# One scan over zero-separated segments, the state kept in place, and a new order of work in a kernel that mixes a 2-D FFT filter with an S5 state space

## The chip, the cores and the metric

The kernel runs on one core of one Trainium2 chip. The metric is the device time of one execution in microseconds (us). "Span" is the length of the one profiled execution; in all runs the recorded time of an execution is its span plus about 1.7 us.

The engines are named as the profile names them: PE (matmul), PEld (weight load, overlaps PE), DVE (VectorE), ACT (ScalarE), POOL (GpSimd), SP (queues DMAs).

## The reference

The inputs are `x` (2048 x 1024, bf16), spectral weights, and the tables of an S5 layer with 1024 complex states. The output mixes two branches by a gate for each row.

```python
g = sigmoid((x * gate_w).sum(-1, keepdims=True))
a = irfft2(rfft2(x) * (w_r + 1j * w_i))              # spectral branch
Lam_bar = exp(dt * Lam)                              # S5 branch, P = 1024 states
Bu = x @ B_bar.T                                     # complex
h[t] = Lam_bar * h[t-1] + Bu[t]                      # over 2048 time steps
b = 2.0 * (h @ Cmat.T).real + x * Dskip
out = g * a + (1 - g) * b
```

## The kernel before

The state branch is cut into 16 **units** `unit(c, q)`: 256 time steps (`c` = 0 to 7) times four blocks of 128 states (`q` = 0, 1). A unit is 64 matmuls into PSUM (the "B product", tile `psu`), an eviction by ACT into `u`, then DVE work: rotate by a table so that the complex recurrence becomes a real one, scan, rotate back. The result `h` waits in one of six buffers until the C products that read it are done.

```python
def b_unit(c, q):
    u = up.tile([P, 4, 2, TC], BF16, name="u")             # two buffers; TC = 256
    for j2 in range(2):
        psu = psU.tile([P, 2, 2, TC], FP32, name="psu", tag="psu")   # psU: two buffers
        ...                                                # 32 matmuls of 128x256
        nc.scalar.copy(out=u[:, 2 * j2:2 * j2 + 2], in_=psu)
    return u

def unit(c, q):
    u = b_unit(c, q)
    ...                                                    # rotate: su, u (4 DVE operations)
    for j in range(4):
        jb = 4 * q + j
        rb = r_sb[:, jb:jb + 1].to_broadcast([P, TC])
        for ri in range(2):
            nc.vector.tensor_tensor_scan(out=u[:, j, ri, :], data0=rb, data1=u[:, j, ri, :],
                                         initial=(0.0 if c == 0 else carry[:, jb, ri:ri + 1]),
                                         op0=ALU.mult, op1=ALU.add)
    ...                                                    # carry for the next 256 steps (3 small ones)
    h = halloc(sh, BF16)                                   # six buffers, 3 + 3
    ...                                                    # rotate back: sg, h (4 DVE operations)
    hs[c, q] = h
```

The spectral branch is a generator, `gfnet`. Its stages are a first transform, then sixteen **W steps** (PE `ps_s`, ACT, DVE multiply by W, PE `ps_is`, ACT, DMA to DRAM), then an inverse stage. `pull(budget)` runs it for so many us of PE work; between pulls the source puts units in. The W loop fetches one step ahead:

```python
X3_next = s2w(0)
Ccol = fixup()
for b in range(16):
    X3 = X3_next
    if b + 1 < 16:
        X3_next = s2w(b + 1)
    psc = psA.tile([P, 2, K], FP32, name="ps_is1", tag="ps")
    ...
```

A C product of 128 rows, `c_gemm(tb)`, multiplies the two `h` tiles of its time range (`q` = 0 and 1) by the C tables into the PSUM tile `ps_y`. Four row blocks have their C products done **early**, before the spectral branch can deliver them; they go to DRAM and come back as `yl` in a "late" finish. `finish` takes eight matmuls of the last transform (`ps_id`), evicts them by ACT into a gated-output buffer `eo`, forms sum and difference `ga` on DVE, adds the state branch and writes the rows out.

```python
def c_gemm(tb):
    psy = psA.tile([P, D], FP32, name="ps_y", tag="ps")
    ...                                       # 32 ps_y matmuls of 128x512, 8 small ones by dgD
def early(tb):
    psy = c_gemm(tb)
    for hf in range(2):
        ye = fft["gq"].tile([P, K], FP32, name="ye", tag="ga")
        nc.scalar.activation(out=ye, in_=psy[:, K * hf:K * (hf + 1)], func=ACT.Copy, scale=omg[:, tb:tb + 1])
        nc.sync.dma_start(out=y_dram[tb, hf], in_=ye)

def finish(tb, psy=None):
    pse = psU.tile([P, 2, K], FP32, name="ps_id", tag="psu")     # shares the two psU buffers
    ...
    eo = raw[:, D * (4 + tb % 2):D * (5 + tb % 2)].rearrange("p (c k) -> p c k", c=2)
    nc.scalar.activation(out=eo, in_=pse, func=ACT.Copy, scale=gB[:, tb:tb + 1])
    ga = fft["gq"].tile([P, 2, K], BF16, name="ga")
    nc.vector.tensor_add(out=ga[:, 0], in0=eo[:, 0], in1=eo[:, 1])
    nc.vector.tensor_sub(out=ga[:, 1], in0=eo[:, 0], in1=eo[:, 1])
    ...                                       # add yl (late) or ps_y; DMA out
```

The last stage is a loop in which each pass has a finish, a late finish while there are any, and a unit:

```python
    pull(5.0);  unit(0, 0)
    pull(10.0); unit(1, 0)
    pull(11.6)
    pull(13.0); unit(0, 1)
    pull(14.6); unit(1, 1)
    pull(7.0);  unit(2, 0)
    pull(1e9)                                 # rest of the spectral stages
    unit(2, 1)
    after_ic()
    for tb in range(NEARLY):                  # NEARLY = 4
        early(tb)
        if tb % 2:
            for q in range(2):
                unit(3 + tb // 2, q)
    todo = list(range(NEARLY, 16)); late = list(range(NEARLY))
    for c in range(3 + NEARLY // 2, 8):
        for q in range(2):
            tb = todo.pop(0)
            finish(tb, c_gemm(tb))
            if late:
                finish(late.pop(0))
            unit(c, q)
```

The source order is not the engines' order: a scheduler places the instructions of each engine under the limits of the buffers. Where this text speaks of "the static list", it means the instruction list of PE as built.

## Time and profile before

Three runs before the prediction gave a median of 422.48 us (422.34 to 424.92). The profiled execution has a span of 424.3 us.

| stage | where it is read | before, us |
|---|---|---|
| first W step starts (first `ps_s` by K table) | times of the tile | 104.5 |
| first and last inverse product of the W steps (`ps_is` from X) | times of the tile | 123.7, 171.9 |
| last product of the inverse stage starts (`ps_is` from raw) | times of the tile | 198.8 |
| end of the span | page | 424.3 |

The page's busy times, with the share of the span and the number of instructions:

```profile
PE 373.0 (88%) x2569; PEld 237.2 (56%) x2601; DVE 301.6 (71%) x525; ACT 167.1 (39%) x210; POOL 20.9 (5%) x52
```

PE has 51 us without work. Where these lie is seen in the windows (stretch, its length, then busy us and instructions of PE, PEld, DVE, ACT, POOL, granted clock, DMA share, GB/s):

```profile
core 0: us, PE busy (x) PEld busy (x) DVE busy (x) ACT busy (x) POOL busy (x), PEclk, DMA share, GB/s
160.00:180.00 20.00, 15.17 (x91) 9.08 (x93) 19.85 (x35) 11.22 (x17) 0.00 (x0) 0.96 0.52 171
...
240.00:260.00 20.00, 19.38 (x133) 12.66 (x133) 19.69 (x30) 3.14 (x3) 0.00 (x0) 1.00 0.00 1
260.00:280.00 20.00, 14.44 (x77) 8.44 (x78) 15.21 (x25) 3.03 (x3) 0.00 (x0) 0.83 0.16 53
...
300.00:320.00 20.00, 18.23 (x121) 11.61 (x122) 17.09 (x28) 4.14 (x4) 0.00 (x0) 1.00 0.16 53
```

In the W stage DVE is full and PE is not. At 260 to 280 neither is full: PE loses 5.6 us and also part of its clock. In the later passes each window still lacks 1.8 us of PE. The waits (who waited for what, us in all, times, longest):

```profile
ACT raw L480 <- DVE ga L483: 23.4, 4, 9.1
...
PE psu L205 <- ACT raw L480: 11.6, 4, 6.0
DVE h L235 <- PE ps_y L457: 11.2, 1, 11.2
```

The timeline around the hole (start, length, engine, what, and in brackets the idle time before it and its releaser):

```profile
263.80 0.42 DVE L483 TENSOR_TENSOR ga<-raw 128x512 bf16<-128x512 bf16 x1
...
264.34 1.11 ACT L480 ACTIVATE raw<-ps_id,gB 128x1024 bf16<-128x1024 f32 x1 [9.14 <-DVE ga L483]
...
265.50 6.07 PE L205 MATMUL psu<-xT,BT 128*128 128x256 bf16 x32 [6.02 <-ACT raw L480]
```

Read from the bottom: a B product waits 6.02 us for a PSUM buffer, which the finish's `ps_id` holds until ACT has evicted it; ACT waited 9.14 us for DVE's `ga`, which reads the same `eo`. After the hole the 32 matmuls take 6.07 us where 3.5 to 3.7 are usual.

```profile
L378 PE MATMUL ps_is<-X,raw x16: 379/390/607, 123.7 to 171.9; 128*128 128x512 bf16 x16
```

The second of these groups are the scans of the first time range, which start from zero and not from a carry. The eight scans of a unit overlap at their ends: eight busy times of 0.73 us take 5.24 us.

### The profile page before, as it was taken

To read this page: it belongs to the slowest core of one execution; us is meant where nothing else is said; L and a number is where in the kernel's file an instruction comes from. 1 tells how busy PE (TensorE), PEld (TensorE's weight loads), DVE (VectorE), ACT (ScalarE), POOL (GpSimd) and SP (SyncE) were. 2 spreads that over 40 slices of the span, in tenths; PEclk is the share of its full clock that TensorE was granted. 3 is DMA by queue.
4 is the path that set the end of the run, shared out by engine and by line. 5 is a ranking of instruction groups with operands and counts; after the bars stand their busy time and mean duration, and the time that the engine had idled before them with its cause. 6 is when DMAs were issued, how large, how long until landed. Compare 5 with 4: busy or idle time off the path is not lost.

```text
span 424.3 us, 6481 instructions
## 1 busy us (share of the span) xinstructions
PE 373.0 (88%) x2569; PEld 237.2 (56%) x2601; DVE 301.6 (71%) x525; ACT 167.1 (39%) x210; POOL 20.9 (5%) x52
## 2 busy tenths in 40 slices
PE   4769888986988998699999994998898999999993
PEld 4737555554855454477455853655565576544441
DVE  3963597192998999999077499597979789862211
ACT  2778887761227667478122211212212022011111
POOL 7100011150000000000000000000000000000000
PEclk9969999998889999999999999799999999999998
DMA  7999913999106886484312000213020100000010
GB/s 214 331 188 184 231 74 91 230 214 210 52 27 224 249 248 222 130 249 129 141 49 75 26 2 0 66 35 101 0 100 25 51 25 2 25 26 25 26 49 25
DMA packets 58078, 46.38 MB, mean 109 GB/s; under 512 B 38720, under 2 KB 43200, under 8 KB 57664
## 3 DMA queue, kind: packets, MB, share of 16 engines
q1 hardware_dynamic: 57616, 45.94, 39.1%
q0 software_dynamic: 352, 0.02, 0.7%
q8 instruction: 20, 0.33, 0.3%
q14 instruction: 10, 0.08, 0.1%
q10 hardware_dynamic: 80, 0.01, 0.0%
HBM read 22.87 MB, written 14.69 MB: 89 GB/s over the span
## 4 chain that ended last, share of the span: by engine, by line
PE 46%; DVE 26%; DMA 11%; ACT 7%; issue 6%; SPq 2%; POOL 1%; ACTq 0%; DVEq 0%; POOLq 0%
PE ps_y L457 19%; PE psu L205 10%; DVE u L224 9%; PE ps_fd L253 6%; PE ps_id L477 3%; DMA BT<-in_A_x_dram 3%; ACT X L256 3%; DVE h L235 2%; DVE t L366 2%; DMA BT<-in_B_B_im_dram 2%; DVE u L217 2%; PE ps_is L395 2%; DVE sg L234 2%; PE ps_is L397 1%; DMA turn_scratch<-A 1%
## 5 line engine op out<-in xcount | busy, mean ns | idle before, releaser
L205 PE MATMUL psu<-xT,BT 128*128 128x256 bf16 x1024 | 128.0, 280 | 17.1 <-ACT raw L480 11.6
L205 PEld LDWEIGHTS <-BT 128*128 128x128 bf16 x1024 | 102.0, 100 | 41.1 <-issue 16.7
L457 PE MATMUL ps_y<-CT,h 128*128 128x512 bf16 x496 | 114.7, 379 | 0.8
L457 PEld LDWEIGHTS <-h 128*128 128x128 bf16 x512 | 49.3, 98 | 54.4 <-ACT ZT L399 0.2
L224 DVE TENSOR_TENSOR_SCAN u<-r_sb,carry,u 128x256 bf16<-128x256 f32 x112 | 74.5, 732 | 0.0
L480 ACT ACTIVATE raw<-ps_id,gB 128x1024 bf16<-128x1024 f32 x16 | 17.8, 1114 | 119.6 <-PE ps_id L477 96.2
L207 ACT CAST u<-psu 128x1024 bf16<-128x1024 f32 x32 | 32.2, 1011 | 51.1 <-PE psu L205 40.6
L216 DVE TENSOR_TENSOR su<-u,tab 128x2048 bf16<-128x2048 bf16 x16 | 19.6, 1225 | 35.5 <-ACT u L207 35.1
L253 PE MATMUL ps_fd<-G_sb,preT 128*128 128x512 bf16 x123 | 31.7, 398 | 4.9 <-ACT X L256 4.1
L477 PE MATMUL ps_id<-raw,ZT 128*128 128x512 bf16 x124 | 29.4, 379 | 0.2
L482 DVE TENSOR_TENSOR ga<-raw 128x512 bf16<-128x512 bf16 x16 | 6.7, 420 | 31.3 <-ACT raw L480 31.3
L235 DVE TENSOR_TENSOR h<-u,tab 128x2048 bf16<-128x2048 bf16 x16 | 19.5, 1219 | 11.2 <-PE ps_y L457 11.2
L253 PEld LDWEIGHTS <-preT 128*128 128x128 bf16 x128 | 18.7, 146 | 15.4 <-issue 8.9
L256 ACT CAST X<-ps_fd 128x1024 bf16<-128x1024 f32 x16 | 20.7, 1305 | 10.1 <-PE ps_fd L253 10.1
L383 ACT CAST C<-ps_is 128x1024 bf16<-128x1024 f32 x16 | 16.2, 1014 | 15.0 <-PE ps_is L381 12.9
L217 DVE TENSOR_TENSOR u<-u,tab 128x2048 bf16<-128x2048 bf16 x16 | 19.6, 1223 | 0.4
L362 ACT CAST X<-ps_s 128x1024 bf16<-128x1024 f32 x16 | 16.3, 1018 | 8.8 <-PE ps_s L360 8.8
L234 DVE TENSOR_TENSOR sg<-u,tab 128x2048 bf16<-128x2048 bf16 x16 | 19.5, 1219 | 0.1
L477 PEld LDWEIGHTS <-ZT 128*128 128x128 bf16 x128 | 12.0, 98 | 12.3
L399 ACT CAST ZT<-ps_is 128x1024 bf16<-128x1024 f32 x16 | 15.4, 1016 | 5.7 <-DMA raw<-turn_scratch 4.5
L498 PE MATMUL pt<-ident,BT 128*128 128x128 bf16 x128 | 11.3, 250 | 6.9 <-DMA BT<-in_A_x_dram 6.9
L491 DVE SCALAR_TENSOR_TENSOR ga<-ps_y,omg,ga 128x1024 bf16<-128x1024 f32 x12 | 15.4, 1284 | 1.1
(182 smaller groups left out, 427.2 us busy)
## 6 DMA issues: line engine op xcount, KB each, us to landing
BT<-in_A_x_dram SPq DMA_DIRECT2D x8, 512.0 KB, 6.3
turn_scratch<-A SPq DMA_DIRECT2D x16, 256.0 KB, 3.2
Bb<-turn_scratch SPq DMA_DIRECT2D x16, 256.0 KB, 3.3
turn_scratch<-C SPq DMA_DIRECT2D x16, 256.0 KB, 3.1
raw<-turn_scratch SPq DMA_DIRECT2D x16, 256.0 KB, 3.6
out_dram<-ga SPq DMA_DIRECT2D x16, 256.0 KB, 2.0
W_b<-in_A_w_r_dram SPq DMA_DIRECT2D x16, 128.0 KB, 3.1
W_b<-in_A_w_i_dram SPq DMA_DIRECT2D x16, 128.0 KB, 2.8
```

What stands on the lines that cost most here:

```text
L205: nc.tensor.matmul(psu[:, j, ri, :], lhsT=BT[jb][:, ri, d8, :], rhs=xT[:, d8, TC * c:TC * (c + 1)], start=(d8 == 0), stop=(d8 == 7))
L207: nc.scalar.copy(out=u[:, 2 * j2:2 * j2 + 2], in_=psu)
L216: nc.vector.tensor_mul(out=su, in0=u[:, :, ::-1, :], in1=bc(1))
L217: nc.vector.tensor_mul(out=u, in0=u, in1=bc(0))
L224: nc.vector.tensor_tensor_scan(out=u[:, j, ri, :], data0=rb, data1=u[:, j, ri, :], initial=(0.0 if c == 0 else carry[:, jb, ri:ri + 1]), o ...
L234: nc.vector.tensor_mul(out=sg, in0=u[:, :, ::-1, :], in1=bc(3))
L235: nc.vector.tensor_mul(out=h, in0=u, in1=bc(2))
L253: nc.tensor.matmul(ps[:, cls, :], lhsT=preT_A[:, cls, d4, j, :], rhs=G_sb[:, cls, d4, :], start=(d4 == 0), stop=(d4 == 3))
L256: nc.scalar.copy(out=X1.rearrange("p r (i c) -> p c r i", c=2), in_=ps.rearrange("p c (r i) -> p c r i", r=2))
L457: nc.tensor.matmul(psy[:, 512 * dh:512 * (dh + 1)], lhsT=hs[c, jb // 4][:, jb % 4, ri, P * tq:P * (tq + 1)], rhs=CT[ri][:, jb, 512 * dh:51 ...
L477: nc.tensor.matmul(pse[:, cls, :], lhsT=ZT_t[:, 4 * cls + i, tb, :], rhs=fft["Gi"][:, 4 * cls + i, :], start=(i == 0), stop=(i == 3))
L480: nc.scalar.activation(out=eo, in_=pse, func=ACT.Copy, scale=gB[:, tb:tb + 1])
```

## The change

The intent: replace eight scans of 256 by two of 1024, with a decay table `rz` whose first entry in each segment is zero (so that no state leaks from one segment into the next) and the carry, multiplied by the decay beforehand, added to the first element; put `h` where `u` was, which frees the memory for `rz`; fetch two W steps ahead; move early C products and a seventh unit into the W stage, where PE has idle time. The diff, cut to its core:

```diff
-    hpA = ctx.enter_context(tc.tile_pool(name="hpA", bufs=3, side="left"))
+    hpA = ctx.enter_context(tc.tile_pool(name="hpA", bufs=NHA, side="left"))     # NHA, NHB = 4, 2
...
+            nc.gpsimd.tensor_copy(out=rz[:, jb, :], in_=r_sb[:, jb:jb + 1].to_broadcast([P, TC]))
+            nc.gpsimd.memset(rz[:, jb, 0:1], 0.0)
...
     def unit(c, q):
-        u = b_unit(c, q)
-        sh = [P, 4, 2, TC]
+        sh = [P, 2, 4, TC]
+        u = halloc(sh, BF16)
...
-        for j in range(4):
-            ...
-            for ri in range(2):
-                nc.vector.tensor_tensor_scan(out=u[:, j, ri, :], data0=rb, data1=u[:, j, ri, :],
-                                             initial=(0.0 if c == 0 else carry[:, jb, ri:ri + 1]), ...)
+        if c:
+            nc.vector.tensor_add(out=u[:, :, :, 0], in0=u[:, :, :, 0], in1=carry[:, :, js])
+        for ri in range(2):
+            seg = u[:, ri].rearrange("p j t -> p (j t)")
+            nc.vector.tensor_tensor_scan(out=seg, data0=rz[:, js].rearrange("p j t -> p (j t)"), data1=seg,
+                                         initial=0.0, op0=ALU.mult, op1=ALU.add)
...
-        h = halloc(sh, BF16)
-        nc.vector.tensor_mul(out=h, in0=u, in1=bc(2))
+        nc.vector.tensor_mul(out=u, in0=u, in1=bc(2))
...
-        X3_next = s2w(0)
+        X3s = [s2w(0), s2w(1)]
...                                       # gt, wp: three buffers in place of two; K3, JP, dgD made later
     def early(tb):
-        psy = c_gemm(tb)
+        psy = c_gemm(tb, psU, "psu")
...
-    pull(10.0)
+    pull(7.5)
+    unit(0, 1)
+    pull(7.5)
     unit(1, 0)
-    pull(11.6)
+    pull(7.5)
+    unit(1, 1)
+    pull(20.0)
+    unit(2, 0)
     pull(13.0)
-    unit(0, 1)
-    pull(14.6)
-    unit(1, 1)
-    pull(7.0)
-    unit(2, 0)
+    early(0)
+    unit(2, 1)
+    pull(8.0)
+    early(1)
+    pull(5.0)
+    unit(3, 0)
     pull(1e9)
-    unit(2, 1)
     after_ic()
-    for tb in range(NEARLY):
-        early(tb)
-        ...
+    early(2)
+    unit(3, 1)
+    early(3)
...
-    for c in range(3 + NEARLY // 2, 8):
+    for c in range(4, 8):
         for q in range(2):
+            unit(c, q)
             tb = todo.pop(0)
             finish(tb, c_gemm(tb))
             if late:
                 finish(late.pop(0))
-            unit(c, q)
```

## The prediction

> **What bounds the kernel now.** Span 424.3 us; the page has PE busy 373.0 us (88%), DVE 301.6 (71%), ACT 167.1. The windows of 20 us show different limits by stage. Transform and W stage, 100 to 200 us: DVE is busy 18 to 19.9 of every 20 us from 120 us on, PE about 17.7; W steps come every 3.1 us (timeline). Early products, 200 to 240: PE is full (19.9). Final loop, 260 to 340: neither is full (PE 14.4 to 18.2); PE's B products wait for a PSUM buffer held by the gated output (waits: psu <- ACT raw 11.6 us, which itself waits 23.4 us for DVE ga): an iteration with a late finish takes 19.6 us for 17.9 us of PE work. From 340 on PE is full, and a tail of 6.9 us ends it.
>
> **What the change does.**
> 1. Scan: eight scans of 256 cost 5.24 us a unit (0.655 us each, back to back). The Trainium skill, "DVE: opcode table, instruction layouts, handler registers and perf-mode slots", section "Datapath and trigger behaviour", says the scan program runs at half throughput. At the 0.96 GHz of the skill's first page that is 0.533 us for 256 elements, so only about 0.12 us a scan is fixed. Estimate: a 1024 scan costs 2.25 us, two of them 4.5: only 0.7 us saved a unit, minus 0.1 for the carry addition; 16 units: about 10 us of DVE. A unit goes from 12.7 to 12.1 us. Most of DVE's saving is NOT on the chain.
> 2. h in place of u: no duration changes; the DVE wait of 11.2 us (h <- ps_y) goes; ACT's eviction now holds the wait.
> 3. Order (read from the static instruction lists): seven units instead of six and two early products stand before the inverse stage ends, so about 8 us more PE work (196 instead of 205 us) has left the last stage, filling PE's idle time (about 19 us in 40 to 200). W steps go two deep, and in mid-loop no unit's DVE work lies between them, so steps should come every 2.3 to 2.6 us instead of 3.1; there DVE (2.2 us a step), ACT (2.25) and DMA (0.79 MB a step, at the 306 GB/s that 251 GB/s at share 0.82 implies) are all close to the limit.
> 4. Against it: 58 more B products stand before the first W step, which should start at about 110 instead of 104.5 us, since the last transform steps, and so the turn through DRAM, come later; dgD (8 x 0.25 us) moves into the busy DVE stretch; constants load later.
>
> **Sum by stage.** The W steps and inverse stage end at 203 us (199.9 before): no gain, but more work done. The last stage then takes about 206 us instead of 224.4: one unit, two early products fewer, late iterations 18.7 instead of 19.6 us, and no 5.6 us hole at 260 to 280 with the slow-clock period after it (32 B products took 6.07 us there, 3.5 elsewhere). Sum 409 us of span; before's timed runs are 1.8 us under its span: about 407.
>
> **Signs.** Scan 2.2 to 2.3 us for 1024; DVE busy down by about 10 us; W steps at 2.3 to 2.6 us; first W step near 110; PE idle after 200 us from 19 down to 10 to 12 us including the tail; PE busy nearly unchanged (365 to 373).
>
> **What would make it wrong.** A scan much cheaper or dearer than half throughput; W steps that are bound by DMA latency or by the SP queue's order; h buffers (six, held from the B product on) stalling ACT and PE; the two-bank PSUM pair shared by early products and units stalling PE. If the middle stage gains as well, 400; if the W stage stalls, 415.

## More of the kernel before

The scan's group and the W steps' inverse products (in the second line: min/median/max ns, then first and last start):

```profile
L224 DVE TENSOR_TENSOR_SCAN u<-r_sb,carry,u 128x256 bf16<-128x256 f32 x112 | 74.5, 732 | 0.0
...
L224 DVE TENSOR_TENSOR_SCAN u<-r_sb,u 128x256 bf16<-128x256 f32 x16 | 10.3, 679 | 0.0
```

A W step takes (171.9 - 123.7) / 15 = 3.21 us.

## The result, and the profile after

Four runs of after have a median of 411.18 us (410.68 to 413.13), against 423.46 us (422.34 to 424.92, four runs) of before. The ratio is 0.9726 (95%: 0.9682 to 0.9771): faster by 2.7%. A ratio compares the means of all runs, so it is not quite the ratio of the medians quoted here; for after these are six (two more took 413.87 and 411.69 us). The output is correct, as in all runs below.

| | before, us | after, us | predicted, us |
|---|---|---|---|
| first W step starts | 104.5 | 109.5 | 110 |
| a W step | 3.21 | 2.65 | 2.3 to 2.6 |
| last product of the inverse stage starts | 198.8 | 203.2 | 203 (stage end) |
| from there to the end of the span | 225.5 | 208.2 | 206 |
| span | 424.3 | 411.4 | 409 |

```profile
PE 369.1 (90%) x2570; PEld 236.8 (58%) x2601; DVE 296.9 (72%) x445; ACT 169.0 (41%) x210; POOL 28.8 (7%) x68
```

The windows of after, for the same stretches:

```profile
core 0: us, PE busy (x) PEld busy (x) DVE busy (x) ACT busy (x) POOL busy (x), PEclk, DMA share, GB/s
160.00:180.00 20.00, 18.45 (x89) 8.09 (x88) 18.25 (x31) 14.30 (x22) 0.00 (x0) 1.00 0.66 219
...
240.00:260.00 20.00, 18.54 (x123) 11.71 (x124) 16.99 (x22) 4.14 (x4) 0.00 (x0) 1.00 0.18 53
260.00:280.00 20.00, 18.61 (x127) 11.86 (x127) 17.02 (x23) 4.14 (x4) 0.00 (x0) 1.00 0.16 53
...
300.00:320.00 20.00, 18.16 (x122) 11.53 (x122) 16.74 (x22) 4.14 (x4) 0.00 (x0) 1.00 0.12 41
```

The large hole is gone, but each of these windows still lacks 1.4 to 1.8 us of PE. The waits:

```profile
ACT raw L485 <- DVE ga L488: 17.3, 4, 4.6
...
PE psu L209 <- ACT raw L485: 5.7, 4, 1.7
```

The wait of DVE for `ps_y` no longer appears. The same spot in the timeline of after:

```profile
247.76 0.42 DVE L488 TENSOR_TENSOR ga<-raw 128x512 bf16<-128x512 bf16 x1
...
248.29 1.11 ACT L485 ACTIVATE raw<-ps_id,gB 128x1024 bf16<-128x1024 f32 x1 [4.26 <-DVE ga L488]
...
249.46 3.65 PE L209 MATMUL psu<-xT,BT 128*128 128x256 bf16 x32 [1.36 <-ACT raw L485]
```

It is the same chain as before, with 1.36 us of loss in place of 6.02. The scan and the W steps:

```profile
L223 DVE TENSOR_TENSOR_SCAN h<-rz,h 128x1024 bf16<-128x1024 f32 x32 | 71.8, 2279 | 0.3
```

```profile
L375 PE MATMUL ps_is<-X,raw x16: 376/379/634, 136.9 to 176.6; 128*128 128x512 bf16 x16
```

So the middle of the kernel ends 4.4 us later (203.2 against 198.8), and the rest is 17.3 us shorter; together 12.9 us. A window from 200 us to the end gives PE 204.81 us busy of 224.30 before, and 198.25 of 211.40 after. Idle time in it fell from 19.5 to 13.2 us, busy time by 6.6 us. Of the 6.6 about 2.5 are the slow clock after the hole (6.07 us for 32 matmuls against 3.5 to 3.7); the rest is work that now runs earlier (after's window still holds the last 3 us of its inverse stage, so less of it shows here than in the list). In the static list, after the last inverse product PE has 204.7 us of work left before and 196.3 after, 8.4 us less (an estimate: matmuls counted in the list, at 0.11 us for 256 columns and 0.217 us for 512, their pitch in the trace). So the 17.3 us are about 8.4 of work moved, 6.3 of idle time and 2.5 of slow clock. In the static list of before no C product stands ahead of the end of the inverse stage; in that of after 64 `ps_y` matmuls do. The trace also shows what did not move: 490 B matmuls start ahead of the end of the inverse stage in before and only 433 in after, and DVE begins the seventh unit at 190.5 us in before and at 206.2 in after. What was gained is two C products (some 14.7 us); almost one unit's B product (57 matmuls, 6.3 us) went the other way.

### The profile page after: what moved, and what is told of

The parts are those of the page before. It is cut to its first block, busy times and chain, and to the rows that moved or that the text cites. A ratio compares the mean times of both kernels' runs of the same rounds, so it can differ in the third digit from the quotient of the medians.

```text
span 411.4 us, 6415 instructions
## 1 busy us (share of the span) xinstructions
PE 369.1 (90%) x2570; PEld 236.8 (58%) x2601; DVE 296.9 (72%) x445; ACT 169.0 (41%) x210; POOL 28.8 (7%) x68
## 4 chain that ended last, share of the span: by engine, by line
PE 51%; DVE 23%; DMA 11%; ACT 8%; issue 4%; SPq 1%; POOLq 1%; ACTq 0%; POOL 0%; DVEq 0%
PE ps_y L462 18%; PE psu L209 16%; DVE h L223 5%; PE ps_fd L249 5%; PE ps_id L482 3%; ACT X L252 3%; DMA raw<-turn_scratch 2%; DMA W_b<-in_A_w_r_dram 2%; DMA Bb<-turn_scratch 2%; DVE h L216 1%; DVE su L215 1%; PE ps_is L392 1%; DVE h L232 1%; DVE sg L231 1%; DMA yl<-y_scratch 1%
## 5 line engine op out<-in xcount | busy, mean ns | idle before, releaser
L209 PE MATMUL psu<-xT,BT 128*128 128x256 bf16 x1024 | 124.0, 276 | 9.0 <-ACT raw L485 5.7
L209 PEld LDWEIGHTS <-BT 128*128 128x128 bf16 x1024 | 100.6, 99 | 30.7 <-issue 7.6
L223 DVE TENSOR_TENSOR_SCAN h<-rz,h 128x1024 bf16<-128x1024 f32 x32 | 71.8, 2279 | 0.3
L485 ACT ACTIVATE raw<-ps_id,gB 128x1024 bf16<-128x1024 f32 x16 | 17.8, 1114 | 113.8 <-PE ps_id L482 96.6
L211 ACT CAST h<-psu 128x1024 bf16<-128x1024 f32 x32 | 32.3, 1010 | 51.7 <-PE psu L209 51.7
L215 DVE TENSOR_TENSOR su<-h,tab 128x2048 bf16<-128x2048 bf16 x16 | 19.6, 1224 | 42.8 <-ACT h L211 42.6
L249 PE MATMUL ps_fd<-G_sb,preT 128*128 128x512 bf16 x122 | 29.8, 381 | 5.1 <-ACT X L252 4.3
L216 DVE TENSOR_TENSOR h<-h,tab 128x2048 bf16<-128x2048 bf16 x16 | 19.6, 1223 | 0.6
L232 DVE TENSOR_TENSOR h<-h,tab 128x2048 bf16<-128x2048 bf16 x16 | 19.6, 1223 | 0.1
L231 DVE TENSOR_TENSOR sg<-h,tab 128x2048 bf16<-128x2048 bf16 x16 | 19.5, 1219 | 0.1
L503 PE MATMUL pt<-ident,BT 128*128 128x128 bf16 x128 | 12.4, 268 | 5.8 <-DMA BT<-in_A_x_dram 5.8
L396 ACT CAST ZT<-ps_is 128x1024 bf16<-128x1024 f32 x16 | 16.1, 1012 | 3.5 <-PE ps_is L394 2.8
L392 PE MATMUL ps_is<-R_sb,raw 128*128 128x256 bf16 x64 | 14.9, 273 | 2.2 <-DMA raw<-turn_scratch 2.1
```

The source lines that it names most:

```text
L209: nc.tensor.matmul(psu[:, j, :], lhsT=BT[4 * q + j][:, ri, d8, :], rhs=xT[:, d8, TC * c:TC * (c + 1)], start=(d8 == 0), stop=(d8 == 7))
L211: nc.scalar.copy(out=u[:, ri], in_=psu)
L215: nc.vector.tensor_mul(out=su, in0=u[:, ::-1], in1=bc(1))
L216: nc.vector.tensor_mul(out=u, in0=u, in1=bc(0))
L223: nc.vector.tensor_tensor_scan(out=seg, data0=rz[:, js].rearrange("p j t -> p (j t)"), data1=seg, initial=0.0, op0=ALU.mult, op1=ALU.add)
L231: nc.vector.tensor_mul(out=sg, in0=u[:, ::-1], in1=bc(3))
```

## The experiments

The theory at the start was that the order (with the pool of the early products) gives the gain, that the scan gives a little, and that `h` in place is free. Rivals: the scan gives the gain by relieving DVE; or the W depth does. Edits are against after (names that begin with a) or before (names that begin with b). One combination could not be had: before with the long scan alone. The build refuses a scan over a two-level operand, so the scan needs the new layout, and with `u` and `h` apart the decay table leaves less room than the 32 KB a partition that the C tables need.

### a_old: after without the order

Before's order of units, its early products' pool, its W depth and its `h` pools; the new scan and `h` in place stay.

```diff
-NHA, NHB = 4, 2
+NHA, NHB = 3, 3
-        X3s = [s2w(0), s2w(1)]
+        X3s = [s2w(0)]
-        psy = c_gemm(tb, psU, "psu")
+        psy = c_gemm(tb)
...                                       # gt, wp: two buffers; pulls, units, early products as in before
```

> The changed kernel with the order of units, the depth of the W steps (one), their two buffers and the early products' pool and place of the kernel before; what remains of the change is the long scan with its layout, h in place of u, and the later constants. Theory (the order and depth carry most of the gain, the scan a part of it): DVE-bound units lose 0.7 us each only where DVE or the late finish bounds, some 4 units in the W stage and 4 to 5 in the final loop: 417 us (414 to 420). Rival one (the gain is the scan's 10 us of DVE): 411 to 413. Rival two (the scan is off the chain everywhere): 421 to 424.

Measured: 444.27 us (443.51 to 444.77), ratio to before 1.0481 (1.0427 to 1.0535). The parts that were thought free or gainful, without the order, make the kernel 4.8% slower than before. ACT waits 38.2 us for `ps_y` before it can evict a B product into an `h` buffer. The expectation fell, and a second question opened: what does `h` in place cost?

### a_scan8: after with the eight short scans

```diff
-        if c:
-            nc.vector.tensor_add(out=u[:, :, :, 0], in0=u[:, :, :, 0], in1=carry[:, :, js])
-        for ri in range(2):
-            ...one scan of 1024 by rz
+        for j in range(4):
+            for ri in range(2):
+                nc.vector.tensor_tensor_scan(out=u[:, ri, j, :], data0=rb, data1=u[:, ri, j, :],
+                                             initial=(0.0 if c == 0 else carry[:, ri, jb:jb + 1]), ...)
```

> The changed kernel with eight scans of 256 in place of two of 1024, all else kept. Theory: about 0.7 us a unit comes back where DVE bounds (units before the first W products, the late iterations of the final loop, which go from 19.4 to about 20 us): 416 to 418 us. Rival one (the gain is the scan's): 420 to 423. Rival two (scan off the chain): 411 to 412.5. In each case DVE busy rises by 10 to 13 us and a scan of 256 again takes 0.68 to 0.73 us.

Measured: 414.96 us (412.71 to 416.54), ratio 0.9791 (0.9719 to 0.9863). DVE's busy time rose by 6.0 us to 302.9, not by 10 to 13, and the time lies in none of the three expected ranges. The ratios differ by 0.65%, with overlapping intervals (together they allow from nothing to about 1.5%), so the times don't resolve what the scan is worth. The traces give an idea: the four late passes are 19.9 us long here and 19.4 in after (first rotations from 234.12 to 313.58 us, and from 234.88 to 312.56), 1.8 us in all.

### a_w1: after with W steps one deep

```diff
-        X3s = [s2w(0), s2w(1)]
+        X3s = [s2w(0)]
-            if b + 2 < 16:
-                X3s.append(s2w(b + 2))
+            if b + 1 < 16:
+                X3s.append(s2w(b + 1))
```

> The changed kernel with the W steps one deep (buffers still three). Theory (depth hides the chain product, eviction, multiplication, product): steps go from 2.65 us back to about 3.0, 415 to 418 us. Rival (steps are faster only because no unit's DVE work lies between them; DMA or DVE bounds them): still 2.6 to 2.7 us a step, 410 to 412.5 us.

Measured: 410.72 us (410.13 to 412.01), ratio 0.9695 (0.9644 to 0.9747); nothing is lost: the time is the rival's. But the W steps do slow down, as the theory said:

```profile
L375 PE MATMUL ps_is<-X,raw x16: 376/389/586, 132.2 to 179.1; 128*128 128x512 bf16 x16
```

A step is back at (179.1 - 132.2) / 15 = 3.13 us. But they start 4.7 us earlier, and the slower loop holds more filler: its static list has 74 B and 32 C matmuls between the first and last inverse product, where after's has 42 and 21, and PE's work after the inverse stage is 191.6 us, not 196.3. A faster W loop holds less of the work that has to be done anyway.

### a_early: early products moved behind the inverse stage

```diff
-    early(0)
     unit(2, 1)
-    pull(8.0)
-    early(1)
-    pull(5.0)
-    unit(3, 0)
+    pull(13.0)
     pull(1e9)
     after_ic()
+    early(0)
+    early(1)
+    unit(3, 0)
```

> The changed kernel with the first two early products and unit (3,0) moved after the inverse stage, as the kernel before had them. Theory (they filled PE idle time in the W stage, about 14.7 us of PE work for the two, 7 for the unit): the last stage grows by 15 to 21 us, the W stage shrinks by 3 to 7 us; 421 to 427 us. Rival (they delay the W steps as much as they save later): 409 to 414 us.

Measured: 412.64 us (411.72 to 413.37), ratio 0.9735 (0.9683 to 0.9788). The run doesn't test its question: in the static list 64 `ps_y` matmuls stand ahead of the inverse stage all the same, and the trace shows them there (63 are recorded). The scheduler had hoisted them, since their pool allows it. So the source position of the early products isn't what counts.

### b_inpl: before with h in place alone

```diff
-        u = up.tile([P, 4, 2, TC], BF16, name="u")
+        u = halloc([P, 4, 2, TC], BF16)
...
-        h = halloc(sh, BF16)
-        nc.vector.tensor_mul(out=h, in0=u, in1=bc(2))
+        nc.vector.tensor_mul(out=u, in0=u, in1=bc(2))
```

> The kernel before with h in place of u alone (the six h buffers are taken from the B product's eviction on). Theory (this is what made the old order with the long scan 20 us slower: the eviction of the seventh unit waits until the first early products have freed a buffer, so no B product of a seventh unit can fill the inverse stage): 436 to 446 us, with 30 us or more of ACT's evictions waiting for ps_y. Rival (the long scan, which can't be broken up between W steps, cost those 20 us): 421 to 425.

Measured: 435.18 us (433.54 to 436.57), ratio to before 1.0231 (1.0162 to 1.0299); the median lies a hair under the expected range, and the expected wait of at least 30 us is there:

```profile
ACT h L207 <- PE ps_y L456: 38.8, 4, 12.0
```

With `h` apart only the back rotation has to wait for a free `h` buffer (11.2 us once). In place, the eviction of the B product takes the buffer, so it is held from the start of the unit; each late eviction also delays the unit's DVE work (two of DVE's waits for it are 6.46 and 8.28 us). PE's own waits show where it loses: 6.2 us at the start of the inverse stage, for data that turn through DRAM, and 5.28 and 5.05 us for ACT's `raw`, the chain of before, now with two large holes (14.66 of 20 us busy at 260 to 280, where before has 14.44, and 14.85 at 300 to 320, where before has 18.23). That the held buffers cause all three is argued, not shown. Most of a_old has the same picture. That a_old is still about 9 us slower than b_inpl (both medians, on two chips) stays open: the scan, the layout or the later constants in that order.

### b_ord: before with the order and the pool alone

Eight scans, `u` and `h` apart, W steps one deep, two buffers: all as in before. Only the order of the source and the early products' pool are after's.

```diff
-        psy = c_gemm(tb)
+        psy = c_gemm(tb, psU, "psu")
...                                       # pulls, units and early products in after's order
-    for c in range(3 + NEARLY // 2, 8):
+    for c in range(4, 8):
         for q in range(2):
+            unit(c, q)
             tb = todo.pop(0)
             ...
-            unit(c, q)
```

> The kernel before with the changed order of units and early products and the early products on the pool of the B products; eight scans, u and h apart, W one deep with two buffers, constants as before. Theory (order and pool carry the gain, scan 2 to 4 us, depth nothing): 412 to 416 us. Rival (the gain needs the scan or the third buffers): 418 to 424.

Measured: 412.95 us (411.65 to 413.21), as expected, ratio 0.9714 (0.9665 to 0.9764). After's is 0.9726. The whole gain is there without the scan, without `h` in place and without the W depth. The large hole is gone here too; the small waits of after remain:

```profile
PE psu L205 <- ACT raw L480: 7.1, 4, 2.1
```

Its W steps run from 127.0 to 176.4 us, its inverse stage ends at 203.0 us, and PE's work after it is 193.1 us.

### b_psU: before with the early products' pool alone

```diff
     def early(tb):
-        psy = c_gemm(tb)
+        psy = c_gemm(tb, psU, "psu")
```

> The kernel before with one word changed: the early products take their PSUM tiles from the pool of the B products. The static list then has the first two inside the W stage. Theory (they fill PE's idle time there; the last stage has 5 us less PE work in the list): 416 to 419 us. Rival (the pool is not what matters, the order of units is): 421 to 424.

Measured: 422.35 us (420.52 to 424.37), ratio 0.9943 (0.9884 to 1.0001). The expectation of a larger gain fell. The early products do move ahead (64 `ps_y` before the end of the inverse stage, 199.9 us of work after it instead of 204.7), but the hole comes back elsewhere: PE is busy 13.93 of 20 us at 240 to 260, and the wait of `psu` for ACT is again 11.6 us.

### a_psA: after with the early products back on the old pool

```diff
     def early(tb):
-        psy = c_gemm(tb, psU, "psu")
+        psy = c_gemm(tb)
```

> The changed kernel with the early products back on the pool of the transform tiles, all else kept. The static list then has no product of C before the inverse stage. Theory (the pool is what lets them fill the W stage and free the h buffers early): 422 to 432 us. Rival (it does not matter): 410 to 413.

Measured: 430.73 us (429.89 to 432.56), ratio 1.0145 (1.009 to 1.0199), as expected. No C product stands ahead of the inverse stage, and PE has nothing to do while the data turns through DRAM:

```profile
core 0: us, PE busy (x) PEld busy (x) DVE busy (x) ACT busy (x) POOL busy (x), PEclk, DMA share, GB/s
...
160.00:180.00 20.00, 11.85 (x47) 4.25 (x48) 20.00 (x37) 12.76 (x20) 0.00 (x0) 1.00 0.62 212
180.00:200.00 20.00, 11.08 (x71) 7.64 (x73) 2.09 (x5) 9.29 (x12) 0.00 (x0) 0.74 0.63 187
```

One line of pool choice is worth some 19 us in after's order (430.73 against 411.18, medians of different rounds; the ratios to before are 1.0145 and 0.9726), and in before's order 0.6%, which is within the noise. Why is it so much with `h` in place? The early products are what frees `h` buffers for the next units; on the W steps' pool they can't run among the W steps. The run shows the consequence; that reason is read from the code.

### b_loop: before with the last loop turned

The unit is put ahead of the finishes, as after has it.

```diff
         for q in range(2):
+            unit(c, q)
             tb = todo.pop(0)
             finish(tb, c_gemm(tb))
             if late:
                 finish(late.pop(0))
-            unit(c, q)
```

> The kernel before with the final loop turned: the unit stands ahead of the finish in each pass, nothing else. Theory (the hole of 5.6 us at 260 to 280 and the slow clock behind it came from the finish standing ahead of the unit whose DVE work it waits behind; it is a large part of what the new order gained): 414 to 419 us, no PE idle over 3 us between 200 and 400. Rival (the order gained by filling the W stage with a seventh unit and two early products): 421 to 424 us.

Measured: 427.45 us (426.78 to 427.96), ratio 1.0071 (1.0024 to 1.0117). The expectation fell: turned alone, the loop costs 0.7%. It trades the hole for a larger one. The timeline:

```profile
303.60 5.24 DVE L224 TENSOR_TENSOR_SCAN u<-r_sb,carry,u 128x256 bf16<-128x256 f32 x8
...
310.59 0.41 DVE L483 TENSOR_TENSOR ga<-raw 128x512 bf16<-128x512 bf16 x1
...
311.12 1.11 ACT L480 ACTIVATE raw<-ps_id,gB 128x1024 bf16<-128x1024 f32 x1 [13.62 <-DVE ga L483]
...
312.29 5.07 PE L205 MATMUL psu<-xT,BT 128*128 128x256 bf16 x32 [10.71 <-ACT raw L480]
```

It is the chain of before once more: ACT's `raw` waits for DVE's `ga`, and `ga` stands in DVE's list behind the scans of a whole unit. PE is busy 9.23 of 20 us there. The pool, the turned loop and `h` in place, each alone on before, gain nothing that counts or lose. That made the chain itself the suspect.

### a_eo: after, the late finish on the other gated-output buffer

The two `eo` buffers go by `tb % 2`. In each pass `tb` and the late one (4 and 0, 5 and 1, ...) have the same parity, so both finishes of a pass use one buffer, and the second has to wait for the `ga` of the first.

```diff
-        eo = raw[:, D * (4 + tb % 2):D * (5 + tb % 2)].rearrange("p (c k) -> p c k", c=2)
+        eb = (tb + (psy is None)) % 2
+        eo = raw[:, D * (4 + eb):D * (5 + eb)].rearrange("p (c k) -> p c k", c=2)
```

> The changed kernel; the gated output of a late finish goes to the other of the two buffers, so that ACT need not wait for DVE's additions of the finish before it. The four passes with a late finish take 19.3 us each for 17.9 us of PE work. Theory (two rings bind them at once: PE and ACT through that buffer, and DVE through its wait of 2.7 us for the second half of the early product's load, which has one buffer): passes stay at 19.2 to 19.3 us, the time at 410 to 412 us, ACT's wait for ga (17 us) nearly gone. Rival (the buffer alone binds): 17.9 us a pass, 404 to 407 us.

Measured: 405.05 us (402.98 to 407.58), ratio to before 0.9547 (0.9495 to 0.9599), against 0.9726 for after. The rival, that the buffer alone binds, was right. The waits of PE for ACT's `raw` are gone, and the windows fill up:

```profile
core 0: us, PE busy (x) PEld busy (x) DVE busy (x) ACT busy (x) POOL busy (x), PEclk, DMA share, GB/s
...
240.00:260.00 20.00, 19.89 (x137) 13.09 (x138) 16.98 (x22) 5.57 (x6) 0.00 (x0) 1.00 0.16 53
260.00:280.00 20.00, 19.89 (x140) 13.38 (x141) 16.93 (x24) 4.36 (x5) 0.00 (x0) 1.00 0.18 54
```

The timeline at the spot where before and after had their waits:

```profile
240.61 7.15 PE L209 MATMUL psu<-xT,BT 128*128 128x256 bf16 x64
240.81 1.11 ACT L486 ACTIVATE raw<-ps_id,gB 128x1024 bf16<-128x1024 f32 x1 [0.61 <-PE ps_id L482]
...
243.58 0.42 DVE L488 TENSOR_TENSOR ga<-raw 128x512 bf16<-128x512 bf16 x1
```

ACT evicts the second `ps_id` 2.8 us ahead of DVE's `ga`, no longer behind it, and the B product runs through: 64 matmuls in 7.15 us. From 200 us to the end PE is now idle for 7.4 us (201.20 less 193.79), 5.7 less than in after, where the four waits summed to 5.7 us; the medians differ by 6.1. (The two profiled spans differ by 10.2, but 3.8 of these lie ahead of the end of the inverse stage, where the edit changes nothing.) DVE's passes hardly became shorter: the first rotation of a unit starts at 231.05, 250.31, 269.55, 288.61 and 307.70 us, 19.2 us apart, against 19.4 in after. DVE still waits 10.7 us in four passes for the load of `yl`; with that load cut to one in a_eoybf (below) the passes are 17.8. So DVE falls behind PE by some 1.3 us a pass, without holding PE up, and makes it up afterwards: its next three passes are 14.5 us apart, where after's are 15.9 to 16.1.

### a_ybf: after, early products kept in bf16

One load and one addition in place of two in a late finish; `y` is rounded to bf16.

```diff
-    y_dram = dram.tile([NEARLY, 2, P, K], FP32, name="y_scratch")
+    y_dram = dram.tile([NEARLY, P, D], BF16, name="y_scratch")
...
-            for hf in range(2):
-                ye = fft["gq"].tile([P, K], FP32, name="yl", bufs=1)
-                nc.sync.dma_start(out=ye, in_=y_dram[tb, hf])
-                nc.vector.tensor_add(out=ga[:, hf], in0=ye, in1=ga[:, hf])
+            ye = fft["gq"].tile([P, D], BF16, name="yl", bufs=1)
+            nc.sync.dma_start(out=ye, in_=y_dram[tb])
+            nc.vector.tensor_add(out=o, in0=ye, in1=o)
```

> The changed kernel with the early products kept in bf16, so that one load and one addition of 128x1024 take the place of two of each. The wait of DVE for the second load (11.5 us in four passes) goes. Theory (the other ring, through the gated output's buffer, still binds, a little shorter): passes of 18.6 to 18.9 us, 408 to 410 us. Rival (the load alone binds): 17.9 us a pass, 404 to 407 us.

Measured: 410.68 us (409.96 to 411.07), ratio 0.9671 (0.9619 to 0.9723), not to be told from after. DVE's wait for the load of `yl` (11.5 us in after) is gone, and yet the passes stay 19.2 to 19.3 us long. Both expectations fell: time taken from DVE at this place became a wait for ACT.

### a_eoybf: both

```diff
+        eb = (tb + (psy is None)) % 2     # as in a_eo
...                                       # and y_dram, ye, yl in bf16, as in a_ybf
```

> Both of the last two. Theory: PE alone binds, 17.9 us a pass, four times 1.4 us less: 405 to 406.5 us (0.985 to 0.988 of the changed kernel). If another ring binds: above 408.

Measured: 404.29 us (402.43 to 405.66, six runs), ratio 0.9521 (0.9482 to 0.9561). A little better than expected. Now DVE's passes are 17.8 us long, the length of PE's work in a pass (17.9), but the time isn't distinguishable from a_eo's: PE had already been full. It beats both kernels, by 4.8% over before; a_eo does nearly the same with one index changed and no rounding.

## Why the prediction was right or wrong

The time, 411.18 us, lies between the two outer cases that the prediction named (400 and 415) and 4.2 us above the predicted 407.

**Right: the gain is in the order, not in the scan.** The prediction put nearly all of the gain into work moved out of the last stage and into the removed hole. b_ord shows it: 0.9714 with the order and the pool alone. That "most of DVE's saving is NOT on the chain" holds too: taking it back (a_scan8) costs 0.65% by the ratios, which is not clear of noise. One rival was not run: a_eo's index alone on before. So it is not shown that the order is the only way to remove the hole.

**Right: the sums by stage.** First W step 109.5 (predicted 110), end of the middle 203 (203), work after it 196.3 (196). The middle didn't gain. The sum is right, but one of its parts is not: "one unit, two early products fewer" in the last stage. Two early products fewer is what ran; of the units, after has almost one more there (433 B matmuls ahead of it, against before's 490). The 8 us are the difference of the two.

**Right: the scan's cost.** The prediction took "half throughput" from the Trainium skill, "DVE: opcode table, instruction layouts, handler registers and perf-mode slots", section "Datapath and trigger behaviour". The trace agrees: a scan of 1024 with constant initial value has a mean of 2279 ns; those of 256 with constant initial value (the first units, `c` = 0) 679 ns. (2279 - 679) / 768 = 2.08 ns an element: two cycles at 0.96 GHz, the clock that the skill's page "Trainium Kernel Development and Optimization" gives in its section "NeuronCore Architecture". Two long scans take 4.48 us where eight short ones take 5.24: 0.76 us saved a unit against 0.7 predicted. But not all of it is length: eight short scans that start from zero take 4.76 us when nothing comes between them (second unit of a_scan8 and of b_ord). So 0.48 us come from reading no carry as initial value, and only 0.28 from scans that are longer and fewer.

**Right in the whole, mis-sized: the late passes.** "Late iterations 18.7 instead of 19.6 us" failed. They took 19.4 us (su at 234.88 to 312.56 us, four passes): 0.2 saved each, not 0.9. Four times 0.7 us is 2.9 us, a little more than the 2.4 us by which the span exceeds the predicted 409. The prediction had seen the chain (`psu` for ACT's `raw` for DVE's `ga`) and taken the hole for it; a_eo shows that the same chain, at 1.3 to 1.7 us a pass, was what still set the length of a pass, and that it is a matter of one buffer. The starts of the first and the fourth of these passes (timeline of DVE; 58.25 us for three), and then the chain of after in order of time, from the end of a unit's DVE work by `ga` and `raw` to the B product:

```profile
234.88 1.23 DVE L215 TENSOR_TENSOR su<-h,tab 128x2048 bf16<-128x2048 bf16 x1 [1.72 <-ACT h L211]
...
293.13 1.22 DVE L215 TENSOR_TENSOR su<-h,tab 128x2048 bf16<-128x2048 bf16 x1
```

The chain:

```profile
266.06 0.68 DVE h L234
266.75 0.34 DVE ga L487
267.08 0.34 DVE ga L488
...
267.53 1.12 ACT raw L485
...
268.70 3.67 PE psu L209 x32
```

**Mis-sized: the offset between span and time.** "Before's timed runs are 1.8 us under its span" used one profiled execution that was slower than the median (426.04 us of recorded time). A recorded time is its own span plus 1.7 us in every kernel here: 411.4 and 413.13, 401.2 and 402.98. After's profiled execution was again the slowest of the four quoted, and the median is only 0.2 us below its span. This makes another 1.6 us; the two terms, 2.4 and 1.6, leave 0.2 of rounding in the 4.2.

**Wrong: the W depth as a part of the gain.** Steps of "2.3 to 2.6 us" came out at 2.65, close. But a_w1, with steps of 3.13 us, loses nothing: what the loop gains in speed it loses as room for filler. The prediction's own sum had "no gain" for the middle, so the number wasn't harmed, but its list of what the change buys was.

**Wrong: `h` in place as free.** "No duration changes" is true of the instructions. The reservation about six buffers stood under what could go wrong, without a price: it is 2.3% in before's order (b_inpl). In after's order the wait doesn't appear, and it buys the memory for the decay table, not time.

**Wrong: DVE busy down by about 10 us.** It fell by 4.7 us (301.6 to 296.9). The scans' busy time fell from 84.8 us (74.5 in the group shown, 10.3 for the 16 from zero) to 71.8, and the 14 carry additions took 2.7 us. Small preparations took about 2 us more. The groups together fell by about 8 us; the other 3 are overlap: a moment in which two instructions of different groups overlap counts in both groups but once on the page, and there was less of it (24.4 us instead of 27.8). It did not matter for the time.

**Right: PE's idle time.** After 200 us it went from 19.5 to 13.2 us; "10 to 12" was 1.2 us too good, again the late passes. PE's clock followed: the skill, "TensorE: Matmul & The Clock Gate", section "What's actually happening", says that an idle window of about 3.4 us halves the rate until about 3.4 us of work have passed. The traces agree roughly: 32 matmuls took 6.07 us after a wait of 6.02 (before) and 5.07 after one of 10.71 (b_loop), with a pitch of 0.213 us in place of 0.109 for the first 5.0 and 3.0 us, but 3.5 to 3.7 in after, behind waits of 1.3 to 1.7 us or none.

**Left open.** Which part of the unit order matters (the pool and the turned loop without it were not run together); why a_old is 9 us behind b_inpl; the scan's share within the noise of a_scan8; what a_eo's index alone would do to before.

## What to carry to other kernels

When two finishes of one pass share a buffer through an index such as `tb % 2`, look at which indices meet in a pass: here equal parities made two buffers act as one, and another index was worth 1.8% where the rewrite of scan, memory and order had given 2.7%. Test the parts of a combined change both alone and taken away: the pool alone gained 0.6%, within the noise, and the turned loop alone lost 0.7%, but with the order of units they gave the whole gain, and the part that gave the change its name gave 0.65% by the ratios, not clear of noise. A stage that gets faster only helps when what it was hiding doesn't have to run somewhere else.

## What the Trainium skill lacked or had wrong

- "DVE: opcode table, instruction layouts, handler registers and perf-mode slots" gives the scan's rate, which the runs confirm (2.08 ns an element), but no page gives its time as an instruction: a mean of 679 ns for 256 and 2279 ns for 1024 elements from a constant initial value, so about 0.15 us fixed; with the carry, read from memory, as initial value it was 732 ns, 53 more. Nor is the way to restart it within one instruction there (zeros in the multiplier).
- "Perfetto Trace Analysis", section "Optimizing Scalar/DVE Operations", gives about 60 ns for DVE on SBUF as the overhead of an instruction, and about twice that as profiled latency because the end overlaps with the next instruction. For back-to-back scans from zero the traces agree: they start 0.58 us apart (a_scan8), of which 256 x 2.08 = 533 ns is streaming, leaving 0.05 us. With the carry as initial value they start 0.643 us apart, which leaves 0.11; no page gives this price of some 0.06 us.
- The same section advises breaking up instructions where an unsaturated engine causes bubbles on another. Here DVE (72% busy) caused PE's bubbles, and one buffer index removed the waits in question (5.7 us to none) without breaking up anything: in a_eo DVE was nearly as late (passes of 19.2 us instead of 19.4) and PE did not wait for it. That two buffers can act as one through the index that picks them is on no page.
- "TensorE: Matmul & The Clock Gate", section "What's actually happening", held roughly (6.07 us for 32 matmuls after a wait of 6.02 us), but its idle window of about 3.4 us is no safe limit: in b_loop a wait of only 2.5 us (PE idle until 372.5 us) was followed, three matmuls later, by some 3.4 us at half rate (a pitch of 0.427 us for 512 columns in place of 0.216), while one of 2.2 us in before was not.
